# Q and K of two heads stacked in the partitions, scores from 64-row matmuls on both halves of the array

## The chip, the cores and the metric

One core of a Trainium2 chip runs the whole program. The metric is device time in microseconds (us); the time before is the median of three runs. Engines are named as in the profile: PE is TensorE (PEld its weight loads), DVE is VectorE, ACT is ScalarE, POOL is GpSimd, SP is SyncE, which issues DMAs.

## The reference

Causal attention with a multiplicative decay, then two MLPs. Batch 4, 8 heads, 576 positions, head size 64; 2304 tokens, model width 512, hidden width 2048.

```python
scores = scale * np.matmul(q, k.transpose(0, 1, 3, 2))
cum = np.cumsum(np.log(np.clip(f, 0.0001, 1.0)), axis=-1)
scores = np.where(causal, -1000000000.0, scores + cum[:, :, :, None] - cum[:, :, None, :])
attn = np.exp(scores - np.max(scores, axis=-1, keepdims=True))
attn = attn / (np.sum(attn, axis=-1, keepdims=True) + 1e-09)
x = np.matmul(attn, v)          # heads side by side: 2304 x 512
h = x @ moe_w_in;  y = (h * sigmoid(1.702 * h)) @ moe_w_out
h = y @ moe2_w_in; out = (max(h, 0) + alpha * min(h, 0)) @ moe2_w_out
```

## The kernel before

Operands of a matmul are split into a high part, rounded to fp32r, and a low part, the rest; a product is then high x high + high x low + low x high, three fp32r matmuls in place of a plain fp32 one.

Attention runs in 32 units (`seq`, line 830). A unit is a pair of heads of one batch and a range of queries: the first sixteen have queries 0 to 256, the others 256 to 576 (320 queries, keys 0 to 576). `prep` (line 479) loads q and k so that 64 partitions hold q's head dimension and the other 64 k's, both heads side by side in the free dimension; DVE transposes blocks of 32x32, one instruction per head (line 496). ACT casts the high parts, DVE or POOL subtracts the low ones (helpers at lines 343 and 348), each on 64 partitions. KB and QB hold low above high and high above low, so one 128-row matmul gives two of the three products; KA and QA hold a second copy of the high parts in rows 0 to 63 and three more rows with cumulated decay, ones and the negated row maximum, so that a 67-row matmul gives the third product and all that is added to it.

`chunk` (line 568) finds the row maxima: for each query tile of 128 and each head one 66-row matmul (line 599), a masked max on DVE (line 602), and then a transpose of the maxima on PE (line 617), which ACT or DVE negate into QA (lines 625, 627). The last 64 queries of both heads share one tile through `z`. `chunk2` (line 632) computes transposed scores for each key tile (lines 654 and 655 for two heads in one PSUM bank, 666 and 667 with a bank for each head), exponentials on ACT (658, 670), a causal mask on POOL (674) and the products with v, in plain fp32 where there are at most 256 queries (lines 686, 692), else in split form (715). Line 686 puts two 64-column matmuls on the two column halves of the array (`tile_position=(0, r)`). Then come the normalisation and the write to xr (725 to 747).

As soon as the columns of 256 tokens are there, `mlp1a` (line 779) runs the first 8 of 16 hidden slots of the first MLP on them (lines 758, 800). It needs 8 converted weight slots (`weight`, lines 449 to 474). The other hidden slots (lines 758, 882) and the second MLP (758, 911) follow when the attention's buffers are free.

The order of all of this is made by a planner (`Plan`, line 69). Each operation has estimated costs on the engines that may run it, reads, writes and a priority; the planner picks, at each step, the operation that can start first, and priority only breaks ties. The result is one fixed order per engine. All eight PSUM banks are one pool; `ps_s` (scores, up to 3 banks), `ps_m` (maxima, 2), `ps_v` (output, 3), `ps_h` (hidden, 2) and `ps_y` (MLP output, 2) are only upper limits. All DMAs are issued by SP, in planned order, so a load that waits for its buffer holds back the ones behind it.

## Time and profile before

| | us |
|---|---|
| median of three runs (lowest, highest) | 1099.09 (1098.65, 1100.13) |
| the profiled execution | 1101.62 |
| its span, first to last instruction | 1099.9 |
| PE busy | 1040.2 |
| DVE busy | 745.8 |
| ACT busy | 503.7 |
| POOL busy | 129.1 |

Busy time of PE is of modelled, pipelined matmuls. What an engine is worth in a stretch is read from the stretch: its busy time there, the granted clock of PE, and what it waited for.

### The profile page before, as it was taken

To read this page: it belongs to the slowest core of one execution; us is meant where nothing else is said; L and a number is where in the kernel's file an instruction comes from. 1 tells how busy PE (TensorE), PEld (TensorE's weight loads), DVE (VectorE), ACT (ScalarE), POOL (GpSimd) and SP (SyncE) were. 2 spreads that over 40 slices of the span, in tenths; PEclk is the share of its full clock that TensorE was granted. 3 is DMA by queue.
4 is the path that set the end of the run, shared out by engine and by line. 5 is a ranking of instruction groups with operands and counts; after the bars stand their busy time and mean duration, and the time that the engine had idled before them with its cause. 6 is when DMAs were issued, how large, how long until landed. Compare 5 with 4: busy or idle time off the path is not lost.

```text
span 1099.9 us, 16292 instructions
## 1 busy us (share of the span) xinstructions
PE 1040.2 (95%) x5955; PEld 897.4 (82%) x5955; DVE 745.8 (68%) x1565; ACT 503.7 (46%) x1009; POOL 129.1 (12%) x179
## 2 busy tenths in 40 slices
PE   4797899999989899999999999999999999999997
PEld 2576888899978889998888898788888888898885
DVE  7998988998989888878973449833443434444433
ACT  6787756567667566667752337511210201211111
POOL 5331111213212221000100000300000000000000
PEclk7697898999979979999999999999999999999999
DMA  6555465344453330655653234500100200100001
GB/s 188 133 166 163 143 168 135 84 108 108 94 135 93 90 95 12 201 184 151 215 179 105 77 103 149 170 1 1 67 1 1 68 1 1 34 24 20 1 1 39
DMA packets 86329, 101.95 MB, mean 93 GB/s; under 512 B 35496, under 2 KB 65384, under 8 KB 86248
## 3 DMA queue, kind: packets, MB, share of 16 engines
q1 hardware_dynamic: 86248, 100.90, 32.0%
q8 instruction: 47, 0.77, 0.3%
q14 instruction: 34, 0.28, 0.1%
HBM read 81.54 MB, written 19.02 MB: 91 GB/s over the span
## 4 chain that ended last, share of the span: by engine, by line
PE 70%; DVE 10%; issue 2%; DMA 2%; ACT 1%; SPq 0%; DVEq 0%; ACTq 0%
PE bk L758 30%; PE bk L911 17%; PE bk L882 8%; PE bk L800 5%; PE bk L715 3%; PE bk L666 2%; PE bk L599 2%; PE bk L667 1%; DVE bk L602 1%; DVE T L496 1%; DVE KB L348 1%; DVE el L348 1%; DVE tr L728 1%; PE bk L655 1%; PE bk L686 1%
## 5 line engine op out<-in xcount | busy, mean ns | idle before, releaser
L343 ACT CAST qgh<-qgg 128x512 fp32r<-128x512 f32 (+1 forms) x120 | 69.3, 578 | 338.3 <-DVE qgg L772 314.8
L769 DVE TENSOR_SCALAR qgg<-bk,alpha_sb 128x512 f32<-128x512 f32 (+1 forms) x80 | 55.5, 695 | 166.9 <-PE bk L758 166.9
L758 PE MATMUL bk<-qx,wB 128*128 128x512 f32 (+1 forms) x720 | 156.9, 370 | 0.0
L758 PEld LDWEIGHTS bk<-qx,wB 128*128 128x128 f32 x720 | 125.8, 188 | 24.5
L758 PE MATMUL bk<-xh,wA 128*128 128x256 f32 x576 | 125.2, 297 | 3.1 <-ACT wA L343 2.0
L348 DVE TENSOR_TENSOR qgl<-qgg,qgh 128x512 fp32r<-128x512 f32 (+1 forms) x116 | 75.5, 651 | 67.3 <-ACT qgh L343 58.7
L758 PEld LDWEIGHTS bk<-xh,wA 128*128 128x128 f32 x576 | 100.8, 202 | 5.3 <-ACT wA L343 2.2
L758 PE MATMUL bk<-qx,wA 128*128 128x512 f32 (+1 forms) x480 | 104.3, 369 | 0.0
L758 PEld LDWEIGHTS bk<-qx,wA 128*128 128x128 f32 x480 | 83.9, 188 | 16.4
L602 DVE CUSTOM_DVE_ANT_0 bk<-bk,mask 128x512 f32<-128x512 f32 (+3 forms) x160 | 75.9, 495 | 14.5 <-PE bk L599 11.8
L758 PE MATMUL bk<-xl,wA 128*128 128x256 f32 x288 | 84.6, 294 | 1.1 <-DVE xl L348 1.1
L800 PE MATMUL bk<-gh,wA 128*128 128x256 f32 x576 | 83.7, 288 | 1.8 <-POOL wA L348 0.7
L800 PEld LDWEIGHTS bk<-gh,wA 128*128 128x128 f32 x576 | 76.1, 194 | 3.2 <-ACT gh L343 1.3
L911 PE MATMUL bk<-wA,qgh 128*128 128x512 f32 x288 | 73.7, 395 | 0.2 <-ACT qgh L343 0.2
L348 POOL TENSOR_TENSOR qx<-qxb,qx 128x512 fp32r<-128x512 f32 (+1 forms) x12 | 15.3, 1277 | 431.3 <-ACT qx L343 373.1
L911 PEld LDWEIGHTS bk<-wA,qgh 128*128 128x128 f32 x288 | 53.7, 188 | 13.1 <-ACT qgh L343 0.6
L496 DVE STREAM_TRANSPOSE T<-raw 128x256 f32<-128x256 f32 (+1 forms) x64 | 58.9, 940 | 3.3 <-DMA raw<-in_k_dram 3.0
L758 PEld LDWEIGHTS bk<-xl,wA 128*128 128x128 f32 x288 | 58.2, 202 | 1.6 <-DVE xl L348 1.5
L458 ACT ACTIVATE wc<-wraw 128x512 f32<-128x512 f32 x64 | 43.2, 678 | 27.6 <-DVE wA L348 9.3
L911 PE MATMUL bk<-wB,qgh 128*128 128x512 f32 x216 | 54.5, 392 | 0.0
L882 PE MATMUL bk<-qgh,wB 128*128 128x512 f32 (+1 forms) x240 | 54.3, 368 | 0.0
L758 PE MATMUL bk<-qx,wC 128*128 128x512 f32 (+1 forms) x240 | 53.0, 371 | 0.0
(150 smaller groups left out, 2129.3 us busy)
## 6 DMA issues: line engine op xcount, KB each, us to landing
wraw<-in_moe_w_in_dram SPq DMA_DIRECT2D x32, 512.0 KB
wraw<-in_moe_w_out_dram SPq DMA_DIRECT2D x32, 512.0 KB
xscr<-xr SPq DMA_DIRECT2D x9, 512.0 KB
ypscr<-yp SPq DMA_DIRECT2D x18, 256.0 KB
raw<-in_q_dram SPq DMA_DIRECT2D x16, 288.0 KB
raw<-in_k_dram SPq DMA_DIRECT2D x16, 288.0 KB
raw<-in_q_dram SPq DMA_DIRECT2D x16, 280.0 KB
raw<-in_k_dram SPq DMA_DIRECT2D x16, 280.0 KB
```

The lines of the kernel that those rows point to most:

```text
L343: nc.scalar.copy(dst, src)
L348: E[e].tensor_tensor(dst, a, b, op=ALU.subtract)
L458: plan.add([("ACT", c_act(n))], lambda e: nc.scalar.mul(w.ap, high().bitcast(F32), 2.0 ** -112), [raw], [w], pri)
L496: [("DVE", 1.9 * n)], lambda e, hh=hh: nc.vector.transpose(T.ap[:, hh, :n].rearrange("p (i n) -> p n i", n=nb), raw.ap[:, hh, :nb * D].rea ...
L599: nc.tensor.matmul(pm.ap[:rows, :c1 - c0], l, ka.ap[0:66, hh, c0:c1], start=hh == hhs[0], stop=hh == hhs[-1])
L602: plan.add([("DVE", c_dve(c1 - c0) + 90.0)], lambda e, pm=pm, rows=rows, c0=c0, c1=c1, mk=mk, m0=m0, col=col: nc.vector.tensor_tensor_redu ...
L715: nc.tensor.matmul(pb[hh].ap[:l.shape[1], s0 - q0:n], l, rhs.ap[:w, hh, :m], start=st, stop=sp, skip_group_check=True,)
L758: nc.tensor.matmul(ph.ap[:, :n], wb.ap[:, a, c, :], x(c), start=(c == 0 and i == 0), stop=(c == KT - 1 and i == 2))
L769: plan.add([("DVE", c_dve(n) + 56)], lambda e: nc.vector.tensor_scalar(g.ap[:, :n], ph.ap[:, :n], 0.0, alpha_sb[:, m:m + 1], op0=ALU.min, ...
L800: nc.tensor.matmul(py[d // 2].ap[:, d % 2 * BLK:(d % 2 + 1) * BLK], W1[m].ap[:, a, KT + d, :], g.ap, start=(m == 0 and i == 0 and a == 0 a ...
L882: nc.tensor.matmul(py[d].ap[:, :n], W1[m].ap[:, a, KT + d, :], g.ap[:, :n], start=(m == NA and i_ == 0 and a == 0), stop=(m == NM - 1 and ...
L911: nc.tensor.matmul(py[t].ap, g.ap[:, t * P:(t + 1) * P], wo[:, a, KT * P:], start=(m == 0 and i_ == 0 and a == 0), stop=(m == NM - 1 and i ...
```

## The change

Both heads of a pair are now stacked in the partitions: head 0 in 0 to 63, head 1 in 64 to 127. k and q get tiles of their own, loaded in four 32-partition DMAs each, with runs of 32 floats; only the unit's own queries of q are loaded. One unstrided transpose, one cast and one subtraction on 128 partitions handle k, and the same q. KH, KL, QH and QL hold the parts, three buffers each. DK and DQ hold, in three rows of each half, what is added to the scores (64 rows, the others zero). A score is four 64-row matmuls per head, in turns on the upper and the lower half of the partitions, into two PSUM banks, and each head has its own exponential. The row maxima are two 64-row matmuls per head in the same turns (the second has `ones` as weights); the shared last tile is two 128-row matmuls. The duplicates KA and QA go. The sums come in two DMAs instead of one for units after the fourth, and v's last rows in one instead of two. `ps_s` may have 4 banks. The loads of q and k of the first sixteen units may be issued by ACT. Initial fills run on POOL alone, and v's loads don't wait for them.

The core of the diff:

```diff
+QUEUE = {"SP": "SP", "ACTQ": "ACT"}
...
+    ACTQ = 16
...
-    p_qa = sb("att", "QA", 2, [67, 2 * (S - SPLIT)], F32R)
-    p_z = sb("att", "Z", 2, [66, 192], F32R)
-    p_ka = sb("att", "KA", 2, [67, 2, S], F32R)
-    p_QB = sb("att", "QB", 2, [P, 2, S - SPLIT], F32R)
-    p_KB = sb("att", "KB", 2, [P, 2, S], F32R)
-    p_raw = sb("att", "raw", 1, [P, 2, S * 2])
-    p_T = sb("att", "T", 1, [P, 2, S])
+
+    ones = att.tile([P, 2, P], F32R, name="ones")
+    p_z = sb("att", "Z", 2, [P, P], F32R)
+    p_rk = sb("att", "rk", 2, [P, S])
+    p_rq = sb("att", "rq", 2, [P, S - SPLIT])
+    p_tk = sb("att", "tk", 1, [P, S])
+    p_tq = sb("att", "tq", 1, [P, S - SPLIT])
+
+    p_kh = sb("att", "KH", 3, [P, S], F32R)
+    p_kl = sb("att", "KL", 3, [P, S], F32R)
+    p_dk = sb("att", "DK", 3, [P, S], F32R)
+    p_qh = sb("att", "QH", 3, [P, S - SPLIT], F32R)
+    p_ql = sb("att", "QL", 3, [P, S - SPLIT], F32R)
+    p_dq = sb("att", "DQ", 3, [P, S - SPLIT], F32R)
...
-    ps_s = psum_pool(3)
+    ps_s = psum_pool(4)
...
+    def set_ones(e):
+        nc.gpsimd.memset(ones.bitcast(F32), 0.0)
+        for hh in range(2):
+            nc.gpsimd.memset(ones[64 * hh:64 * hh + 2, 0].bitcast(F32), 1.0)
+            nc.gpsimd.memset(ones[64 * hh:64 * hh + 2, 1, 64 * hh:64 * hh + 64].bitcast(F32), 1.0)
+
+    b_one = Buf()
+    plan.add([("POOL", 600.0)], set_ones, (), [b_one], -87)
...
+        ("dk", p_dk, lambda x: (x.bitcast(F32), x[0:3].bitcast(F32), x[64:67].bitcast(F32)), 3 * S, (0.0, 1.0, 1.0)),
+        ("z", p_z, lambda x: x.bitcast(F32), P, 0.0),
+        ("dq", p_dq, lambda x: x.bitcast(F32), S - SPLIT, 0.0),
...
-            plan.add([("POOL", 0.95 * n + 60.0), ("DVE", n / 0.96 + 68.0)], lambda e, p=p, i=i, view=view, val=val: [
+            plan.add([("POOL", 0.95 * n + 60.0)], lambda e, p=p, i=i, view=view, val=val: [
...
-        for j, src in enumerate((q, k)):
-            for e_ in range(2):
-                o = 64 * j + 32 * e_
-                ln = nb * D - 32 * e_
-                plan.add(DMA(32 * 2 * ln * 4), lambda e, o=o, e_=e_, src=src, ln=ln: nc.sync.dma_start(
-                    raw.ap[o:o + 32, :, 0:ln],
-                    src[b, h0:h0 + 2, 0:n].rearrange("h (p n) d -> p h (n d)", n=nb)[:, :, 32 * e_:32 * e_ + ln],
+        m = n - q0
+        kh, kl, dk, qh, ql, dq = (Buf(x) for x in (p_kh, p_kl, p_dk, p_qh, p_ql, p_dq))
+        fdk, fdq = filled("dk", p_dk), filled("dq", p_dq)
+        for src, p_r, p_t, hi, lo, c0 in ((k, p_rk, p_tk, kh, kl, 0), (q, p_rq, p_tq, qh, ql, q0)):
+            raw, T = Buf(p_r), Buf(p_t)
+            w = n - c0
+            for o in range(0, P, 32):
+                hh, e_ = o // 64, o // 32 % 2
+                d_ = DMA(32 * w * 4 * 1.6)
+                if actq:
+                    d_.append(("ACTQ", d_[0][1], 300.0))
+                plan.add(d_, lambda e, src=src, hh=hh, e_=e_, o=o, raw=raw, w=w, c0=c0: E[e].dma_start(
+                    raw.ap[o:o + 32, 0:w].rearrange("p (n d) -> p n d", d=32),
+                    src[b, h0 + hh, c0:c0 + w, 32 * e_:32 * e_ + 32].rearrange("(n p) d -> p n d", p=32),
                 ), (), [(raw, o)], pri)
-        m = n - q0
-        for hh in range(2):
-            plan.add(
-                [("DVE", 1.9 * n)], lambda e, hh=hh: nc.vector.transpose(
-                    T.ap[:, hh, :n].rearrange("p (i n) -> p n i", n=nb),
-                    raw.ap[:, hh, :nb * D].rearrange("p (n d) -> p n d", d=D)[:, :, 0:32],
-                ), [raw], [(T, hh)], pri,
-            )
-        Tq, Tk = lambda: T.ap[0:64, :, q0:n], lambda: T.ap[64:P, :, :n]
-        Qh, Ql = lambda: QB.ap[0:64, :, :m], lambda: QB.ap[64:P, :, :m]
-        Kh, Kl = lambda: KB.ap[64:P, :, :n], lambda: KB.ap[0:64, :, :n]
-
-        def dup(dst, dap, src, sap, w):
-            def go(e):
-                if e == "SP":
-                    nc.sync.dma_start(dap().bitcast(F32), sap().bitcast(F32))
-                else:
-                    copy(e, dap(), sap().bitcast(F32))
-
-            plan.add([(*DMA(64 * 2 * w * 4)[0], BD), *a_copy(2 * w)], go, [src], [(dst, "h")], pri)
-
-        plan.add(a_copy(2 * n), lambda e: copy(e, Kh(), Tk()), [T], [(KB, "h")], pri)
-        plan.add(a_copy(2 * m), lambda e: copy(e, Qh(), Tq()), [T], [(QB, "h")], pri)
-        dup(ka, lambda: ka.ap[0:64, :, :n], (KB, "h"), Kh, n)
-        dup(qa, lambda: qv(qa.ap[0:64, 0:2 * qw]), (QB, "h"), Qh, m)
+            plan.add([("DVE", 1.13 * w + 70.0)], lambda e, raw=raw, T=T, w=w: nc.vector.transpose(T.ap[:, :w], raw.ap[:, :w]), [raw], [T], pri)
+            plan.add(a_copy(w), lambda e, T=T, hi=hi, w=w: copy(e, hi.ap[:, :w], T.ap[:, :w]), [T], [hi], pri)
+            plan.add(a_sub(w), lambda e, T=T, hi=hi, lo=lo, w=w: sub(e, lo.ap[:, :w], T.ap[:, :w], hi.ap[:, :w].bitcast(F32)), [T, hi], [lo], pri)
...
+            for i in range(2):
+                plan.add(DMA(8 * n), lambda e, i=i: nc.sync.dma_start(
+                    dkv()[:, i, :n].bitcast(F32), cscr[i, r:r + 2, :n]
+                ), [*((b_cum, (p_, i)) for p_ in parts), *fdk], [(dk, i)], pri)
...
+                pms = [Buf(ps_m) for _ in range(2 if w == P else 1)]
+
+                def mm(e, pms=pms, a=a, w=w, c0=c0, c1=c1):
+                    if w < P:
+                        o = pms[0].ap[:, :c1 - c0]
+                        nc.tensor.matmul(o, z.ap, kh.ap[:, c0:c1], start=True, stop=False)
+                        nc.tensor.matmul(o, ones[:, 1], dk.ap[:, c0:c1], start=False, stop=True)
+                        return
+                    for x, y in ((qh, kh), (None, dk)):
+                        for hh in range(2):
+                            r = slice(64 * hh, 64 * hh + 64)
+                            l = ones[r, 0, :w] if x is None else x.ap[r, a - q0:a - q0 + w]
+                            nc.tensor.matmul(pms[hh].ap[:, :c1 - c0], l, y.ap[r, c0:c1], start=x is not None, stop=x is None)
+
+                plan.add([("PE", 2 * c_mm(c1 - c0, P))], mm, [qh if w == P else z, kh, (dk, 0), (dk, 1), b_one, *u["fdk"]], pms, pri)
...
+                for g, hh in enumerate(hhs):
+                    def ev(e, i0=i0, i=i, a=a, w=w, hh=hh, g=g):
+                        d = dq.ap[64 * hh:64 * hh + 3, a - q0:a - q0 + w]
...
+            pss = [Buf(ps_s), Buf(ps_s)]
+
+            def sc(e, pss=pss, a=a, w=w, s0=s0, m=m):
+                for i, (x, y) in enumerate(((kh, qh), (kh, ql), (kl, qh), (dk, dq))):
                     for hh in range(2):
+                        r = slice(64 * hh, 64 * hh + 64)
+                        nc.tensor.matmul(pss[hh].ap[:w, :m], x.ap[r, a:a + w], y.ap[r, s0 - q0:n], start=i == 0, stop=i == 3)
+
+            plan.add([("PE", 4 * c_mm(m, w))], sc, [kh, kl, dk, qh, ql, dq], pss, pri)
+            for hh in range(2):
+                plan.add([("ACT", c_act(m, True))], lambda e, hh=hh, pss=pss, e32=e32, w=w, m=m: nc.scalar.activation(
+                    e32.ap[:w, hh, :m], pss[hh].ap[:w, :m], AF.Exp, scale=0.125
+                ), [pss[hh]], [(e32, hh)], pri)
```

## Rows read from the trace of the kernel before

**Rows 1.** The page: the span in 40 slices, tenths busy, tenths of full clock

```profile
DVE  7998988998989888878973449833443434444433
...
PEclk7697898999979979999999999999999999999999
```

**Rows 2.** Stretches: start:end, length, busy us of five engines, PE clock, DMA share, GB/s

```profile
0.00:165.00 165.00, 128.24 (x850) 106.83 (x850) 145.33 (x402) 116.71 (x235) 44.57 (x72) 0.81 0.58 160
165.00:443.00 278.00, 263.84 (x1919) 246.56 (x1921) 246.40 (x563) 177.51 (x390) 56.66 (x87) 0.94 0.38 94
443.00:493.50 50.50, 49.13 (x409) 48.56 (x407) 44.61 (x95) 36.20 (x78) 1.77 (x1) 1.00 0.65 209
```

**Rows 3.** An instruction of PE: start, length, line, idle before and what ended it

```profile
317.40 0.27 PE L617 MATMUL bk<-ident_r,MX 128*3 128x128 f32 x1 [2.54 <-DVE MX L609]
```

**Rows 4.** Groups of DVE: line, tiles, shapes, count, busy us, mean ns, idle before

```profile
L496 DVE STREAM_TRANSPOSE T<-raw 128x576 f32<-128x576 f32 x32 | 39.6, 1243 | 3.1 <-DMA raw<-in_k_dram 3.0
L348 DVE TENSOR_TENSOR KB<-T,KB 64x1152 fp32r<-64x1152 f32 x16 | 21.7, 1354 | 1.0 <-ACT KB L343 0.6
L496 DVE STREAM_TRANSPOSE T<-raw 128x256 f32<-128x256 f32 x32 | 19.3, 637 | 0.2
L348 DVE TENSOR_TENSOR QB<-T,QB 64x640 fp32r<-64x640 f32 x16 | 13.1, 819 | 0.4
L348 DVE TENSOR_TENSOR KB<-T,KB 64x512 fp32r<-64x512 f32 x16 | 12.4, 777 | 1.1 <-ACT KB L343 0.8
```

**Rows 5.** Groups of DVE with the shapes nearest to the new ones

```profile
L348 DVE TENSOR_TENSOR el<-e,eh 128x640 fp32r<-128x640 f32 x43 | 35.7, 835 | 4.3 <-ACT eh L343 4.0
L348 DVE TENSOR_TENSOR gl<-gg,gh 128x256 fp32r<-128x256 f32 x47 | 20.3, 436 | 1.7 <-ACT gh L343 1.0 <-PE bk L800 0.5
L735 DVE STREAM_TRANSPOSE tr<-rc 128x320 f32<-128x320 f32 x16 | 7.9, 495 | 0.1
L735 DVE STREAM_TRANSPOSE tr<-rc 128x256 f32<-128x256 f32 x16 | 6.8, 426 | 0.0
```

**Rows 6.** Groups of ACT

```profile
L670 ACT ACTIVATE e<-bk 128x320 f32<-128x320 f32 x96 | 35.7, 443 | 9.9 <-PE bk L667 9.6
L343 ACT CAST KB<-T 64x1152 fp32r<-64x1152 f32 x16 | 18.5, 1154 | 0.3
L658 ACT ACTIVATE e<-bk 128x512 f32<-128x512 f32 x16 | 9.5, 596 | 5.6 <-PE bk L655 5.4
```

**Rows 7.** DMA: two stretches as in rows 2; issues of line 489 (min/median/max ns)

```profile
205.50:208.50 3.00, 3.00 (x21) 2.77 (x21) 2.57 (x6) 2.98 (x6) 2.88 (x4) 1.00 0.97 239
195.50:196.50 1.00, 1.00 (x10) 1.00 (x10) 1.00 (x4) 0.00 (x0) 1.00 (x2) 1.00 0.86 195
...
L489 SPq DMA_DIRECT2D raw<-in_k_dram x64: 311/425/1404, 1.7 to 389.8; - x64
```

**Rows 8.** Instructions of PE in order of time, at full clock

```profile
123.39 0.28 PE L758 MATMUL bk<-xh,wA 128*128 128x256 f32 x1
123.60 1.52 PE L686 MATMUL bk<-e,VR 128*64 128x256 f32 x16
125.05 0.39 PE L599 MATMUL bk<-KA,QA 66*128 66x256 f32 x1
...
185.15 0.31 PE L666 MATMUL bk<-QA,KA 67*128 67x320 f32 x1
185.30 0.31 PE L667 MATMUL bk<-QB,KB 128*128 128x320 f32 x1
...
186.42 0.27 PE L655 MATMUL bk<-QB,KB 128*128 128x192 f32 x1
186.53 0.28 PE L654 MATMUL bk<-QA,KA 67*128 67x192 f32 x1
...
191.63 0.81 PE L692 MATMUL bk<-e,VR 128*128 128x192 f32 x4
192.37 0.45 PE L686 MATMUL bk<-e,VR 64*64 64x64 f32 x8
```

More of the change, by code (lines that the diff above doesn't have):

```diff
@@ L127, in run @@
                     bias, port = (*more, 0.0, False)[:2] if len(more) < 2 else more
-                    t = max(t0, free.get(eng, 0.0))
+                    t = max(t0, free.get(QUEUE.get(eng, eng), 0.0))
                     if port:
                         t = max(t, free.get("port", 0.0))
-                    if eng == "SP":
+                    if eng in QUEUE:
                         end = max(t + 1150.0, dma) + dur + 750.0
@@ L144, in run @@
             o.start, o.eng = t, eng
[L145 to L146 removed]
+            if eng in QUEUE:
+                free[QUEUE[eng]] = t + 480.0
                 dma = end - 750.0
@@ L216 @@
     plan = Plan()
-    E = {"PE": nc.tensor, "DVE": nc.vector, "ACT": nc.scalar, "POOL": nc.gpsimd, "SP": nc.sync}
+    E = {"PE": nc.tensor, "DVE": nc.vector, "ACT": nc.scalar, "POOL": nc.gpsimd, "SP": nc.sync, "ACTQ": nc.scalar}
     const = ctx.enter_context(tc.tile_pool(name="const", bufs=1))
@@ L578, in chunk @@
             jobs += [(j, t, a, w, (hh,)) for hh in range(2)] if w == P else [(j, t, a, w, (0, 1))]
-        for ji, (j, t, a, w, hhs) in enumerate(jobs):
+        ji = 0
+        for j, t, a, w in [(j, *x) for j, x in enumerate(tiles)]:
             ext = a + w
@@ new lines, in chunk @@
+                plan.add([("PE", 2 * c_mm(c1 - c0, P))], mm, [qh if w == P else z, kh, (dk, 0), (dk, 1), b_one, *u["fdk"]], pms, pri)
+                for i, pm in enumerate(pms):
+                    col = 32 * (ji + i) + (2 if c0 == 0 else 3)
+                    if w == P:
+                        mk, m0 = mask, 3 * P - t * P + c0
+                    else:
+                        mk, m0 = (mask, 0) if c1 < ext else (mask2, 0)
+                    plan.add([("DVE", c_dve(c1 - c0) + 90.0)], lambda e, pm=pm, c0=c0, c1=c1, mk=mk, m0=m0, col=col: nc.vector.tensor_tensor_reduce(
+                        pm.ap[:, :c1 - c0], pm.ap[:, :c1 - c0], mk[:, m0:m0 + c1 - c0], 1.0, NEG,
+                        ALU.add, ALU.max, accum_out=mx.ap[:, col:col + 1],
+                    ), [b_mask if mk is mask else b_mask2, *fmx], [pm, (mx, col)], pri)
+                    cols.append(col)
@@ L608, in chunk @@
+            if w < P:
                 x, y = cols
-                plan.add([("DVE", 70.0, 0.0, True)], lambda e, x=x, y=y, rows=rows: nc.vector.tensor_tensor(
-                    mx.ap[:rows, x:x + 1], mx.ap[:rows, x:x + 1].bitcast(F32), mx.ap[:rows, y:y + 1].bitcast(F32), op=ALU.max
+                plan.add([("DVE", 70.0, 0.0, True)], lambda e, x=x, y=y: nc.vector.tensor_tensor(
+                    mx.ap[:, x:x + 1], mx.ap[:, x:x + 1].bitcast(F32), mx.ap[:, y:y + 1].bitcast(F32), op=ALU.max
@@ L832 @@
     for i, (b, hp, q0, q1) in enumerate(seq):
-        unit = prep(b, hp, q0, q1, A0 + i - PRE, i < EARLY)
+        unit = prep(b, hp, q0, q1, A0 + i - PRE, i < EARLY, i < ACTQ)
         pend.append((chunk(unit, q0, q1, A0 + i), col0(b, q0) + q1 - q0 if hp == NP - 1 else 0))
```

120 lines of the change are left out of this document (33 added, 87 removed).

## The prediction

> **What bounds the kernel now.** I began with the page's slices: TensorE (PE) runs at full granted clock in nearly all of the later ones, while the first half shows VectorE (DVE) at seven to nine tenths through the first nineteen and PE's clock below full again and again [rows 1]. So there are two kernels in one, and only the first is touched. I cut it into four stretches [rows 2]: A, 0 to 165 us, about the first sixteen units (256 queries); B, to 443 us, the last of the sixteen units with 320 queries; C, to 493.5 us, the rest of the first MLP part, for which PE needs no more attention; then D, the 606 us that are left, MLP alone at full clock [rows 1]. D does not change. C is PE's as well (busy for 49.1 of 50.5 us), so the end of the kernel is D plus whatever it takes PE to get through all work of A, B and C.
>
> What does that work take? In A PE is idle for 165.0 - 128.2 = 36.8 us, and its mean clock of 0.81 costs roughly another 165 x 0.19 = 31 us; so its work is worth about 97 us at 2.4 GHz. In B it is idle for 14 us and the clock costs 278 x 0.06 = 17 us: 247 us of work. C has 49. Together 393 us of work in 493.5: 68 us are lost in A, 33 in B and C. Who makes PE wait? DVE is busy for 88% of A and 89% of B, ScalarE (ACT) for 71% and 64% [rows 2]. A typical loss in B, at 317 us: PE waits 2.54 us for DVE's last row maximum [rows 3], and the slice that follows has a clock of 0.7 in place of 0.9 or more [rows 1]. A is DVE's stage; B is one where PE and DVE are both close to full.
>
> **DVE: what goes and what comes.** Now, per unit of the first kind, two strided transposes of 128x256 (0.637 us each) and two subtractions of 64x512 (0.777 for K; Q has the same shape); of the second kind two of 128x576 (1.243) and two subtractions (1.354 and 0.819) [rows 4]. That is 2.83 and 4.66 us. Afterwards the same values lie on all 128 partitions: transposes of 256 and 256, or 576 and 320 columns, unstrided, and subtractions of the same widths. Unstrided 32x32 transposes take 0.426 (256) and 0.495 us (320); for 576 I extend the line, 0.495 + 256 x 1.08 ns = 0.77. Subtractions take 0.436 (256 columns) and 0.835 (640) [rows 5]; between them 320 gives 0.52 and 576 gives 0.75. So 2 x 0.43 + 2 x 0.44 = 1.73 us and 0.77 + 0.50 + 0.75 + 0.52 = 2.54: 1.10 and 2.12 us less per unit, 17 us in A and 34 in B. In A DVE's share of the initial fills, which I put at 5 us, also moves to GpSimd, idle for 120 of A's 165 us; in B some 4 us come back, from two small copies into z per unit in place of one and one more copy of maxima. DVE's work: A 145 - 22 = 123, B 246 - 30 = 216.
>
> **ACT.** K of a second unit is cast as 64x1152 in 1.154 us [rows 6] and then copied once more for KA; Q likewise, 64x640, by columns some 0.7 each: 3.7 us. One cast of 128x576 and one of 128x320, half the columns each and so about 0.6 to 0.7 and 0.4, replace all four: 2.6 us less per second unit and, by columns, 1.6 less per first one, 67 us in all. Every exponential that covered both heads is split: 0.596 for 512 columns becomes two of 256, which the line through that and 0.443 for 320 puts at 0.39 [rows 6]; 0.19 more, over four such tiles per pair of units and 16 pairs some 10 us. ACT may also issue loads in the first sixteen units. Its price is not in the trace; SP's row has a median of 0.425 us per load [rows 7]. At most half of 128, 64 x 0.42 = 27 us, if none hides behind a running instruction, and nothing if all do. I take 13: ACT in A is then 117 - 26 + 5 + 13 = 109, below DVE. What is queued behind such a load, should it wait for its buffer, are exponentials and casts, and PE behind those; two buffers make that wait rare.
>
> **Loads.** The loads of q and k move 26.1 MB now (both operands, both heads, 256 or 576 rows of 256 bytes, less the 32 columns that the second of two loads skips), at 239 GB/s and a share of 0.97 where they run alone [rows 7]: 26.1 / 0.239 x 0.97 = 106 us of all engines. Afterwards a run is 32 floats, 128 bytes: 4 x 512 runs per first unit, 4 x 896 per second, 90,112 in all. The nearest row is v's: 256-byte runs at 195 GB/s and a share of 0.86 [rows 7], 0.86 x 16 / 762 = 18 ns each. A run of half the size costs between nothing and that, so at most 90,112 x 18 / 16 = 101 us. No dearer than now, and spread over 380 us. Issues: eight instead of four of 0.42 us per unit, and the rows of sums as two instead of one; SP has some 17 us for a second unit (B over 16). At the start v's loads no longer wait on SP for their fill; the rows don't price that, it stays at nothing and no loss, since a wait goes. A load that waits for its buffer still holds back the ones behind it, weights among them.
>
> **PE.** Now a score tile is two full-height matmuls per head: from one start to the next 0.15 us at 320 columns (0.133 at 2.4 GHz and about 0.014 more, 0.147) and 0.11 at 192 [rows 8]; for 64 I take 0.06. Afterwards it is four 64-row matmuls per head, and the row maxima are two instead of one. If the upper and the lower half run at once, a pair costs what one full matmul did and the sum stays. The rows have no row halves, but they have column halves: the 16 matmuls of line 686 for one unit, two for each of the code's four per key tile, 8 of 256 columns and 8 of 128. They are plain fp32 and stream their columns twice: line 692, fp32 and full height, takes 0.74 us for four of 192 columns, 0.185 each, where fp32r takes 0.11 [rows 8]. One after another at 2.4 GHz that is (8 x 512 + 8 x 256) / 2.4 = 2560 ns, 2.56 us; they took 1.45 until the next line starts. So halves do run in pairs, 1.28 us of it, and 0.17 us is lost on the way in and out; the matmul of 256 columns ahead took 0.21 instead of 0.107 + 0.014 = 0.12, another 0.09. A visit to split mode costs 0.26 us. Bounds for the overlap: none (the pairs' time doubles) to 14 ns less per pair than now (147 against 320/2.4 = 133). I take the row of the column halves, full overlap, worth -4 us. What the pairs stream per unit is, second kind, 12 x 0.147 + 4 x 0.11 + 4 x 0.06 + 2 x 0.175 + 2 x 0.23 = 3.25 us, first kind 4 x 0.12 + 4 x 0.11 + 2 x 0.11 + 2 x 0.12 = 1.38: 74 us over all, so overlap matters.
>
> The Trainium skill, "TensorE: Matmul & The Clock Gate", Part 3, gives a measured 3.07 times for four row tiles, so 77% of ideal; it speaks against full overlap. By it the 74 us would grow by 0.3 x 74 = 22 (an estimate from that page), some 16 of it in B, where the sum would come out at 1098; the row of line 686 shows 2.0 for two column halves once the visit is taken off.
>
> How many visits? A second unit has two max steps and five score steps in pairs; scores that follow one another share a visit. Four PSUM banks for scores let two steps stand side by side, so 3 to 7; I take 6. First units: 2 to 4, I take 3.5. A: 56 x 0.26 = 15 us, B: 96 x 0.26 = 25; ends 8 to 17 and 12 to 29.
>
> **The sum.** A is DVE's: 123 / 0.88 = 140, 25 us shorter (10 if only the chain through the maxima counts, 33 if the loads help). PE's 97 + 15 fit in it. B and C: PE has 296 + 25 - 4 = 317 us of work. DVE could finish B in 216 / 0.89 = 243 us, so DVE no longer holds B; PE does. It lost 33 us there; with DVE 12% lighter I take 20 (10 to 33). So 337 instead of 328.5, 8 us longer: PE pays for the visits and DVE's gain in B hardly shows. Net -25 + 8 = -17. The profiled execution took 1101.62 (span 1099.9), 2.5 above the median of 1099.09; both less 17: 1085 and **1082**. Its own range, from the ends of visits and losses: 1064 to 1096.
>
> **Rivals.** First, a larger gain: visits are cheap or few (12 us in B) and PE's loss falls to 10; then B and C take 314, 14 us less, and A 33 less: 1052. For it: in C, with DVE no longer ahead of it, PE was busy for 49.1 of 50.5 us [rows 2]; against: a second unit has seven steps that each want two banks.
>
> Second, slower: the halves do not overlap, or their weight loads come one after another. The pairs' 16 x 3.25 = 52 us in B then go on top (A has 28 us to spare for its 22): 1082 + 52 = 1134. With only the loads in turn, a pair cannot be under 2 x 0.11 (the 0.11 of a 192-column matmul is more than its 192/2.4 = 0.08, so its weights set it [rows 8]): 12 x 0.073 + 4 x 0.11 + 4 x 0.06 = 1.6 us per unit, 25 in B: 1107. It ends slower than before from about 17 us of extra PE work in B on. Against it stands the row of line 686.
>
> Third, PSUM. A max step and a score step now take two banks at once. The MLP accumulators hold two banks and the output of a unit two, so four are left. A score bank was held for 0.30 + 0.44 us, now for 0.60 + 2 x 0.44 = 1.5; the pair of max banks for both reductions. If steps queue for banks, PE idles as in [rows 3] more often: half of A's gain goes (12), B's loss stays at 33 (13): 1107. For it: DVE's reductions of one step can no longer overlap the next step's matmuls. The Trainium skill, "TensorEngine Tiling (Array Packing)", Gotcha 1, says that row tiles may not share a bank, which is why there are two; no row here shows it.
>
> Fourth, loads late: SP's order or ACT's loads stall DVE's transposes. DVE's transposes wait 3.0 us in all for loads now [rows 4]; up to 1 us per unit would be 16 us: 1098.
>
> **How the numbers follow.** Forecast 0.46; larger gain 0.20; no overlap 0.12; banks 0.14; loads 0.08. About 0.2%, 2 us, can be told from no change. Faster: 0.46 + 0.20 and 0.04 from banks and loads, 0.70. Same: 0.08, from those two. Slower: no overlap, and what is left of the two, 0.22. Range 1045 to 1118: it leaves out the best of the larger gains (0.07) and full serialisation (0.08) with a little of the banks.
>
> **What would show it.** Right: transposes at 0.43 to 0.8 us and DVE near 123 us of a shorter A; pairs of 64-row matmuls starting within some ns of each other, and 0.14 us per pair at 320 columns; B and C near 335 us with PE full. Wrong: a pair at 0.22 or 0.29 us; PE idle ahead of the max or score lines on DVE or ACT by more than before; DVE waiting for raw; the granted clock lower in B. The end of the first MLP part at 477 us, against 493.5, would be the sum itself.

## The result, and the profile after

The changed kernel takes 1089.13 us (median; 1084.09 to 1090.33) against 1099.61 us for the kernel before on the same chip: a ratio of 0.9893, with a 95% interval from 0.9857 to 0.9928, so about 1% faster (10.5 us between the medians of four runs each, 11.8 by the ratio). The profiled execution took 1090.33 us with a span of 1088.6, 11.3 us less than the one before. The last matmul of the first MLP part (line 793) ends at 481.4 us; before it was 493.5 (line 800). So all of the gain, 12.1 us in this pair of traces, is in the stretches that the forecast called A, B and C, and the rest is unchanged (607 us, was 606), as it should be.

The slices of the page after, and the three stretches (columns as in rows 2):

```profile
DVE  5878887788879875969963459743534333544433
...
PEclk8887899999999999999999999999999999999999
```

```profile
0.00:165.00 165.00, 128.29 (x1029) 103.88 (x1030) 126.29 (x401) 91.83 (x242) 48.03 (x94) 0.88 0.59 135
165.00:443.00 278.00, 274.83 (x2402) 247.81 (x2402) 225.43 (x581) 155.75 (x433) 51.61 (x83) 1.00 0.28 63
443.00:493.50 50.50, 50.50 (x375) 48.40 (x374) 41.22 (x86) 34.76 (x73) 0.24 (x1) 1.00 0.58 176
```

Beside [rows 1, 2] three things stand out. DVE is lighter in A (126 us, was 145) and in B (225, was 246), about as forecast (123 and 216). Yet PE's idle time in A is 36.7 us, and was 36.8. And in B PE is now busy for 274.8 of 278 us at full clock, where it had lost 14 us to idle time and some 17 to the clock. Worked out as in the forecast, PE's loss in A went from 68 only to 56 us (36.7 idle and 165 x 0.12 for the clock), that in B and C from 33 to 3, and PE's work grew by 29 us, from 393 to 422 (481.4, where the first MLP part ends, less 60). 41 less lost and 29 more work are the 12 us.

The new instructions of DVE (line, tiles, shapes, count, busy us, mean ns), and in B the longest waits of PE, for the maxima and for their negation into QA (total, times, longest), first of the kernel before and then of the changed one:

```profile
L514 DVE STREAM_TRANSPOSE tk<-rk 128x576 f32<-128x576 f32 x16 | 12.1, 757 | 0.0
L357 DVE TENSOR_TENSOR KL<-tk,KH 128x576 fp32r<-128x576 f32 x12 | 9.8, 819 | 0.4 <-ACT KH L352 0.3
L514 DVE STREAM_TRANSPOSE tq<-rq 128x320 f32<-128x320 f32 x16 | 8.0, 502 | 0.0
L514 DVE STREAM_TRANSPOSE tk<-rk 128x256 f32<-128x256 f32 x16 | 6.9, 429 | 0.7 <-POOL KL L357 0.6
```

```profile
PE bk L617 <- DVE MX L609: 5.9, 4, 2.5
PE bk L666 <- ACT QA L625: 3.0, 5, 1.0
PE bk L654 <- DVE QA L627: 2.1, 1, 2.1
PE bk L666 <- DVE QA L627: 1.6, 3, 1.3
```

```profile
PE bk L623 <- DVE MX L614: 1.1, 2, 0.8
```

The instructions answer to [rows 4] and cost about what was forecast from [rows 5] (0.77, 0.75, 0.50, 0.43). The 2.54 us wait of [rows 3] has no counterpart left. Of the 14 us that PE was idle in B, 12.6 were waits in the chain through the maxima; 1.1 us of these are left, and no wait for the negated maxima is among B's any more.

PE in the middle of B: start, length, line, operands, shape, count of the group (the two matmuls of a pair start within some 10 ns of each other and stand in one line):

```profile
289.36 0.28 PE L751 MATMUL bk<-xl,wA 128*128 128x256 f32 x1
289.48 0.28 PE L751 MATMUL bk<-xh,wA 128*128 128x256 f32 x1
289.69 0.44 PE L598 MATMUL bk<-KH,QH 64*128 64x384 f32 x2
289.96 0.34 PE L598 MATMUL bk<-DK,ones 64*128 64x384 f32 x2
290.14 0.31 PE L659 MATMUL bk<-QH,KH 64*128 64x320 f32 x2
290.29 0.30 PE L659 MATMUL bk<-QL,KH 64*128 64x320 f32 x2
...
291.88 0.40 PE L598 MATMUL bk<-KH,QH 64*128 64x512 f32 x2
...
293.07 0.39 PE L751 MATMUL bk<-xh,wA 128*128 128x256 f32 x1
```

Twelve pairs of 320 columns take 291.88 - 290.14 = 1.74 us, 0.145 each: a pair costs what one full-height matmul did [rows 8], so here the halves overlap fully. Going in is seen too: 0.21 us from the last matmul on full height to the first pair, where 256 columns take 0.12.

Last, the weights of the first MLP. First the kernel before, then after: SP's loads of them, and the casts that end the conversion of each half slot (count, min/median/max ns, first and last start):

```profile
L454 SPq DMA_DIRECT2D wraw<-in_moe_w_in_dram x11: 368/384/569, 3.1 to 141.9; - x11
L343 ACT CAST wA<-wc x15: 597/617/621, 13.1 to 114.6; 128x512 fp32r<-128x512 f32 x15
```

```profile
L471 SPq DMA_DIRECT2D wraw<-in_moe_w_in_dram x11: 385/408/792, 27.1 to 157.0; - x11
L352 ACT CAST wA<-wc x16: 601/619/631, 46.7 to 122.2; 128x512 fp32r<-128x512 f32 x16
```

This is one of two places where A's gain went (the other is full_height's, below). The first load of weights is issued at 27 us instead of 3, behind 24 loads of q and k on SP instead of 4, and the conversions begin at 47 instead of 13. The first six units are done by 60 us (71 before), but the next four take 12 to 18 us each, with eleven of the sixteen casts beside them. The sixteenth unit's row of line 728 (735 before) comes at 169 us, 8 earlier than before, while lines 751 and 793 have started 350 matmuls by 165 us instead of 390; 40 x 0.12 = 5 us of that is owed later. Three of the kernels below (in_turn, twice, twice_late) have nearly the same order in A; their traces give 166 to 170 us and 345 to 373 matmuls, so a single trace is good to a few us here.

### The profile page after: what moved, and what is told of

Read it like the earlier page. It is cut to its first block, busy times and chain, and to the rows that moved or that the text cites. A ratio compares the mean times of both kernels' runs of the same rounds, so it can differ in the third digit from the quotient of the medians.

```text
span 1088.6 us, 17737 instructions
## 1 busy us (share of the span) xinstructions
PE 1040.8 (96%) x6531; PEld 885.5 (81%) x6531; DVE 696.0 (64%) x1560; ACT 448.3 (41%) x1041; POOL 124.8 (11%) x196
## 3 DMA queue, kind: packets, MB, share of 16 engines
q10 hardware_dynamic: 10608, 1.28, 0.8%
## 4 chain that ended last, share of the span: by engine, by line
PE 69%; DVE 4%; ACT 1%; issue 1%; DMA 1%; SPq 0%; ACTq 0%
PE bk L751 30%; PE bk L904 18%; PE bk L875 8%; PE bk L793 5%; PE bk L659 3%; PE bk L708 2%; PE bk L598 1%; PE bk L685 1%; DVE wraw L480 0%; DVE wB L357 0%; PE bk L679 0%; DMA wraw<-in_moe_w_in_dram 0%; DVE wc L483 0%; DVE qgg L762 0%; DVE qgl L357 0%
## 5 line engine op out<-in xcount | busy, mean ns | idle before, releaser
L751 PE MATMUL bk<-xh,wA 128*128 128x256 f32 x576 | 122.6, 293 | 2.6 <-DVE wA L357 1.5
L751 PEld LDWEIGHTS bk<-xh,wA 128*128 128x128 f32 x576 | 95.7, 192 | 10.4 <-issue 3.8
L751 PE MATMUL bk<-xl,wA 128*128 128x256 f32 x288 | 81.9, 284 | 1.1 <-DVE xl L357 1.1
L663 ACT ACTIVATE e<-bk 128x320 f32<-128x320 f32 (+3 forms) x224 | 65.2, 365 | 29.9 <-PE bk L659 28.2
L751 PEld LDWEIGHTS bk<-xl,wA 128*128 128x128 f32 x288 | 55.4, 192 | 1.3 <-DVE xl L357 1.3
L667 POOL TENSOR_SCALAR_AFFINE_SELECT e<-e 128x256 f32<-128x256 f32 (+1 forms) x80 | 32.7, 421 | 199.4 <-ACT e L663 175.8
```

The source lines that it names most:

```text
L663: plan.add([("ACT", c_act(m, True))], lambda e, hh=hh, pss=pss, e32=e32, w=w, m=m: nc.scalar.activation(e32.ap[:w, hh, :m], pss[hh].ap[:w, ...
L667: plan.add([("POOL", 150.0 + 0.82 * 2 * w, 0.0, True)], lambda e, e32=e32, w=w: nc.gpsimd.affine_select(e32.ap[:w, :, :w], e32.ap[:w, :, : ...
L751: nc.tensor.matmul(ph.ap[:, :n], wb.ap[:, a, c, :], x(c), start=(c == 0 and i == 0), stop=(c == KT - 1 and i == 2))
```

## The experiments

Each kernel ran beside the kernel before on its chip. Times are set against the changed kernel by these ratios: the difference of two ratios times 1100 us. The changed kernel's own interval is 4 us to each side, and with the other kernel's a difference is good to 4 or 5 us; smaller ones are not told apart. full_height, in_turn, twice, twice_late and long_runs keep the planned order. In the others the edit lets the planner make another order for all engines, so more changes than the edit names.

| kernel | median us | ratio, 95% interval | against the changed kernel, us |
|---|---|---|---|
| changed | 1089.13 | 0.9893 [0.9857, 0.9928] | |
| full_height | 1066.91 | 0.9712 [0.9682, 0.9742] | -20 |
| in_turn | 1090.90 | 0.9916 [0.9884, 0.9948] | +3 |
| two_banks | 1098.00 | 0.9974 [0.9959, 0.9989] | +9 |
| twice | 1090.74 | 0.9891 [0.9872, 0.9910] | 0 |
| twice_late | 1097.27 | 0.9957 [0.9938, 0.9977] | +7 |
| w1_first | 1083.20 | 0.9843 [0.9824, 0.9862] | -6 |
| sp_only | 1097.30 | 0.9971 [0.9956, 0.9986] | +9 |
| long_runs | 1079.18 | 0.9789 [0.9768, 0.9810] | -11 |
| w1_first_sp_start | 1087.22 | 0.9860 [0.9836, 0.9884] | -4 |
| w1_first_long_runs | 1078.09 | 0.9791 [0.9770, 0.9812] | -11 |
| w1_first_stay | 1078.85 | 0.9783 [0.9766, 0.9800] | -12 |
| w1_first_stay_long | 1094.19 | 0.9947 [0.9928, 0.9967] | +6 |

**What a visit to split mode costs: full_height.**

```diff
-                    for hh in range(2):
-                        r = slice(64 * hh, 64 * hh + 64)
-                        nc.tensor.matmul(pss[hh].ap[:w, :m], x.ap[r, a:a + w], y.ap[r, s0 - q0:n], start=i == 0, stop=i == 3)
+                    nc.tensor.matmul(pss[i % 2].ap[:w, :m], x.ap[:, a:a + w], y.ap[:, s0 - q0:n], start=i < 2, stop=i > 1)
```

(The maxima likewise.)

> The changed kernel with each pair of 64-row matmuls replaced by one full-height matmul of the same columns (the scores of a pair of heads are summed, and the two banks share the four terms, so the values are other ones); all other instructions and their order stay. It leaves out the visits to the split mode and nothing else. If a visit costs 0.26 us and there are 96 of them from 165 to 443 us, as forecast, the end of the kernel comes 25 us earlier there, about 1064 against 1089. If the visits are as many and as dear as the trace of the changed kernel suggests (61 in that stretch, about 0.2 us each, so 12 us), about 1077. If the visits are hidden, or if a pair costs less than a full-height matmul, 1089 or more. From 0 to 165 us PE is idle for 37 us, so there I expect no more than 3 us from it.

It took 20 to 22 us less. PE's order in the changed kernel has 91 visits, 30 in A and 61 in B (forecast: 56 and 96), so a visit costs 0.22 to 0.24 us of the kernel's time, good to 0.05. My price was 0.26; the count was what I had too high. And visits in A are not covered by idle time: the first MLP part ends at 458.6 instead of 481.4 us, 23 us for 91 visits, 0.25 each with those of A among them. What PE saves in A goes to MLP matmuls that then need not be done later: 396 of them have started by 165 us instead of 350, and the sixteenth unit's row comes at 160 us instead of 169. A and B of this kernel:

```profile
0.00:165.00 165.00, 125.64 (x888) 103.73 (x888) 130.54 (x422) 94.00 (x248) 50.78 (x96) 0.91 0.62 141
165.00:443.00 278.00, 273.73 (x2155) 263.31 (x2156) 238.53 (x606) 169.37 (x465) 52.06 (x81) 0.99 0.31 77
```

Worked out as above, PE's loss is 54 us in A, about the 56 of the changed kernel, and 7 in B instead of 3. So in B some 4 us of what PE saves are lost again to waits and the clock, and the visits cost PE itself somewhat more than this price. The weights come as late here as in the changed kernel (first load at 27 us), so late weights alone do not explain A.

**Whether the halves overlap, and how firmly: in_turn.**

```diff
-                for i, (x, y) in enumerate(((kh, qh), (kh, ql), (kl, qh), (dk, dq))):
-                    for hh in range(2):
+                for hh in range(2):
+                    for i, (x, y) in enumerate(((kh, qh), (kh, ql), (kl, qh), (dk, dq))):
```

(The maxima likewise.)

> The changed kernel with the same 64-row matmuls in another order: within a step all of the upper head's, then all of the lower head's, so that neighbours use the same half of the array. If the two halves really stream at the same time in the changed kernel, that is lost here but for one pair at each turn: about half of the pairs' 3.25 us comes on top for each of the 16 second units, 52 us from 165 to 443 us, less some 10 for the neighbours at the turn, and up to 22 us before that, of which idle PE hides most: 1130 to 1150. If the halves did not overlap, and starts 3 ns apart in the trace were only an artefact of the records, the order makes no difference: 1089.

I was wrong by 40 us or more, and not because the halves don't overlap. PE in this kernel, columns as above:

```profile
290.46 0.45 PE L598 MATMUL bk<-KH,QH 64*128 64x384 f32 x2
...
290.92 0.30 PE L659 MATMUL bk<-QH,KH 64*128 64x320 f32 x1
291.06 0.30 PE L659 MATMUL bk<-QL,KH 64*128 64x320 f32 x1
291.10 0.41 PE L659 MATMUL bk<-QH,KH 64*128 64x320 f32 x1
291.21 0.30 PE L659 MATMUL bk<-QH,KL 64*128 64x320 f32 x1
291.35 0.30 PE L659 MATMUL bk<-QL,KH 64*128 64x320 f32 x1
291.36 0.31 PE L659 MATMUL bk<-DQ,DK 64*128 64x320 f32 x1
...
294.41 0.39 PE L751 MATMUL bk<-xh,wA 128*128 128x256 f32 x1
```

In program order the upper half's four (QH,KH; QL,KH; QH,KL; DQ,DK) come before the lower half's first. But the lower half's QH,KH starts at 291.10, ahead of the upper half's third and fourth (291.21, 291.36): in these rows each half takes its own matmuls in order and does not wait for the other's. The whole visit, two max steps and five score steps, takes 3.95 us here (290.46 to 294.41) and 3.38 in the changed kernel (289.69 to 293.07); one after another on 2.4 GHz its 6656 columns per head would need 2 x 6656 / 2.4 = 5.5 us. So the halves still overlap for the most part, and over the whole kernel the order costs nothing that can be told (+3 us, two runs). The Trainium skill, "TensorE: Matmul & The Clock Gate", Part 3, says that matmuls start strictly in program order without reordering; between two row halves this trace shows otherwise, by 0.1 to 0.3 us.

**PSUM banks: two_banks.**

```diff
-    ps_s = psum_pool(4)
+    ps_s = psum_pool(2)
```

> The changed kernel with two instead of four PSUM banks for the scores, so that no score step can stand beside another one. The rival that steps queue for banks would see its price here: every step waits for the exponentials of the one before (two of 0.3 to 0.45 us), PE changes modes at each of a second unit's steps, some 6 to 7 visits instead of 3.8, 16 x 3 x 0.25 = 12 us from 165 to 443 us, and PE's idle time rises: 1100 to 1115. If four banks are no more than two need, 1089.

Slower by 9 us, a little short of the range. Its stretch B:

```profile
165.00:443.00 278.00, 276.44 (x2346) 240.59 (x2345) 217.99 (x572) 160.56 (x433) 49.98 (x79) 1.00 0.28 63
```

PE is no more idle than in the changed kernel. What rises is the count of visits, from 91 to 118: at full_height's price 27 x 0.23 = 6 us of the 9. So too few banks seem to cost by scattering the score steps, and only little by making PE wait; the rest of the 9 us is not assigned.

**Is A the stage of DVE's throughput? twice, and the same in B: twice_late.**

```diff
-            ... lambda e, raw=raw, T=T, w=w: nc.vector.transpose(T.ap[:, :w], raw.ap[:, :w]) ...
+            ... lambda e, raw=raw, T=T, w=w: [nc.vector.transpose(T.ap[:, :w], raw.ap[:, :w]) for _ in range(2 if not q0 else 1)] ...
```

(`if q0` in twice_late.)

> The changed kernel with each of the 32 transposes of the sixteen first units issued twice (the second writes the same values again): 32 x 0.43 = 13.8 us more on VectorE between 0 and 165 us, the order of everything else kept. If VectorE's throughput bounds that stage, as the forecast had it, the time grows by 13.8 or a little more: 1103 to 1106. My theory now is that it doesn't (VectorE is busy for 126 of 165 us there): most of it goes into holes, and what stands in the chain of a unit counts: 1091 to 1096.

> The changed kernel with each of the 32 transposes of the sixteen second units issued twice (the second writes the same values again): 16 x (0.76 + 0.50) = 20 us more on VectorE, nearly all of it between 165 and 443 us, so that VectorE is as busy there as in the kernel before (245 of 278 us). If PE's loss in that stretch went from 33 to 3 us because VectorE got lighter, a good part comes back: PE idle for 8 us or more there and a clock below 0.97, time 1097 to 1110. If it went because operands are now ready earlier (three buffers, work ahead) and PE's queue never runs dry, VectorE's 33 idle us take it: 1089 to 1092.

In twice, DVE's groups of transposes, and stretch A:

```profile
L514 DVE STREAM_TRANSPOSE tk<-rk 128x256 f32<-128x256 f32 x32 | 14.0, 437 | 1.5 <-POOL KL L357 0.6 <-DMA rk<-in_k_dram 0.3
L514 DVE STREAM_TRANSPOSE tq<-rq 128x256 f32<-128x256 f32 x32 | 13.9, 433 | 0.7
```

```profile
0.00:165.00 165.00, 128.82 (x1024) 102.60 (x1024) 138.64 (x433) 91.91 (x241) 48.35 (x94) 0.89 0.59 135
```

14 us more work on DVE, and no difference in time that can be told. DVE is busy for 77% of A in the changed kernel and for 84% here. So its throughput does not bound A in the changed kernel; that rules out the forecast's reading of the stage after the change, and even my expectation of a few us was too high. The kernel before, with DVE busy for 88%, was not run in this way. In B it is otherwise. In twice_late 20 us more cost 7, good to 4 or 5, and in its trace PE waits more for DVE's maxima (4.2 us in five waits, was 1.1 in two) and is idle for 7.7 us of B instead of 3.2 (B, then the longest of PE's waits in it):

```profile
165.00:443.00 278.00, 270.31 (x2340) 241.53 (x2339) 233.09 (x590) 152.06 (x423) 48.82 (x80) 1.00 0.26 58
```

```profile
PE bk L623 <- DVE MX L614: 4.2, 5, 1.8
```

So DVE's lightness is worth some of what B gained. It is hardly all: PE's clock stays at 1.00, where I expected less than 0.97, and the 30 us don't come back. But the test is not quite a full one, since DVE is busy for 233 us of B here, not for the 245 that I expected and the 246 of the kernel before, and the traced execution (1093.9 us) is one of the faster ones. The others that changed with it (ACT lighter by 22 us in B, three buffers, the order) were not taken apart.

**The weights of the first MLP: w1_first, sp_only, w1_first_sp_start.** In this order:

```diff
-        plan.add(DMA(P * n * 8), lambda e: nc.sync.dma_start(raw.ap.rearrange("p c n t -> p c (n t)"), src), (), [raw], pri)
+        plan.add(DMA(P * n * 8), lambda e: nc.sync.dma_start(raw.ap.rearrange("p c n t -> p c (n t)"), src), (), [raw], pri - 5.5)
...
-    ACTQ = 16
+    ACTQ = 0
...
-        unit = prep(b, hp, q0, q1, A0 + i - PRE, i < EARLY, i < ACTQ)
+        unit = prep(b, hp, q0, q1, A0 + i - PRE, i < EARLY, EARLY <= i < ACTQ)
```

> The changed kernel with one number changed: the loads of the MLP weights get a priority 5.5 lower, so that the first two go out right behind the operands of the first two units, as in the kernel before, and not at 27 us. My theory of the first stage as it stands after the comparison of the traces: VectorE is not what bounds it any more; the conversions of the first MLP weights start at 47 us instead of 13 (their loads stand behind more loads of q and k on SP's queue) and all 16 then fall between 47 and 122 us, so that the units there take 13 to 18 us and PE lacks MLP work to fill its 37 idle us. Then this gives back most of what was missing: the end of the first MLP part goes from 481.6 to about 470 us, and the time to about 1078. Rival: the stage is bound by the chain through the maxima and VectorE whatever the order of conversions: 1087 to 1091. Second rival: the early weight loads delay q and k: units are late at the start, 1092 to 1096.

> The changed kernel with no loads on ScalarE's queue (39 of them in the first stage go to SP instead). If SP's queue is what holds back the weights and with them the first stage, 39 x 0.42 = 16 us more on SP make it worse: 1093 to 1100, the first conversion later than 47 us. If the loads that ScalarE issues are what delays the start (the first logarithm and the casts stand behind them; the first unit ends at 32 us instead of 29), it gets better by about 3 us: 1086. If neither, 1089.

> The changed kernel with the weights' loads early (as in w1_first, 1083) and with ScalarE issuing loads only from the fifth unit on. In sp_only the first logarithm started at 3.7 us instead of 8.6 and the first unit was done at 23 instead of 32 us, but the weights came later still and the sum was worse by 8. If these are two separate causes, both gains add: first unit at 23 to 25 us, first conversion before 30 us, end of the first MLP part 465 to 470, time 1075 to 1080. If the early units are not on the path, because PE's work is what the end waits for and the start only moves idle time, 1081 to 1085.

Loads and casts in w1_first, then in sp_only:

```profile
L471 SPq DMA_DIRECT2D wraw<-in_moe_w_in_dram x11: 368/386/1898, 7.7 to 145.1; - x11
L352 ACT CAST wA<-wc x15: 602/620/647, 19.6 to 116.9; 128x512 fp32r<-128x512 f32 x15
```

```profile
L471 SPq DMA_DIRECT2D wraw<-in_moe_w_in_dram x11: 372/385/1702, 55.1 to 161.6; - x11
L352 ACT CAST wA<-wc x15: 607/619/644, 63.5 to 126.7; 128x512 fp32r<-128x512 f32 x15
```

The order of the three is the order of the times: first load at 8 us, 1083; at 27, 1089; at 55, 1097. On SP 9, 24 and 64 loads of q and k stand ahead of it. The two ends are 14 us apart, well clear of noise; w1_first's own 6 us are only just clear of it. In w1_first the first MLP part ends at 471.9 us (481.4), PE is busy for 135.2 us of A instead of 128.3, and 393 of the first MLP's matmuls have started by 165 us instead of 350. The end of that part came as expected (about 470 us), the time, 1083 for 1078, did not quite. In sp_only, inside its range, SP's queue carries the 39 loads that ACT issues otherwise. It also shows what loads on ACT's queue do at the start. The table load ahead of ACT's first logarithm, and the first exponentials, in the changed kernel and then in sp_only:

```profile
7.29 1.28 ACT L422 ACT_TABLE_LOAD   x1 [3.94 <-DMA rq<-in_q_dram]
25.20 0.38 ACT L663 ACTIVATE e<-bk 128x256 f32<-128x256 f32 x1
```

```profile
2.42 1.28 ACT L422 ACT_TABLE_LOAD   x1
16.65 1.00 ACT L663 ACTIVATE e<-bk 128x256 f32<-128x256 f32 x4
```

The logarithm stands behind loads that ACT has to issue, and the first unit is done at 32 us instead of 23. But w1_first_sp_start, which frees ACT for the first four units, has its first unit at 23 us and is no better than w1_first: 1087, above both of its expected ranges. SP's queue then carries those loads, the conversions begin at 26 us instead of 20, and the sixth unit ends at 71 us in both. So the earlier start by itself bought nothing that can be told.

**The price of 128-byte runs: long_runs and w1_first_long_runs** (the second with w1_first's edit too).

```diff
-                    raw.ap[o:o + 32, 0:w].rearrange("p (n d) -> p n d", d=32),
-                    src[b, h0 + hh, c0:c0 + w, 32 * e_:32 * e_ + 32].rearrange("(n p) d -> p n d", p=32),
+                    raw.ap[o:o + 32, 0:w],
+                    src[b, h0 + hh, c0:c0 + w, :].rearrange("(p n) d -> p (n d)", p=32)[:, 0:w],
```

> The changed kernel with the same loads of q and k in count and bytes, but each partition reads one contiguous run of 1 to 2.3 KB in place of runs of 128 bytes (the operands then hold other elements of q and k, so the values are other ones). It takes the packets of these loads from about 155,000 to under 10,000 and leaves all else in place. If the price of short runs holds anything up (transposes that wait for loads, weights behind them), the first stage gets shorter: 5 us or more, 1084 or less. My theory: the loads are two units ahead, and only a wait or two for them goes: 1086 to 1089.

> w1_first (1083) with the long runs of long_runs in the loads of q and k (so other elements of q and k are read and the values are other ones). long_runs gained 10 us, w1_first 6 to 7. If both do the same thing by two ways, bringing the first MLP weights to their conversions sooner, the second gain is mostly used up: 1079 to 1083. If the early loads and the short runs are two causes (the start of the conversions, and the pace of loads behind them), they add up: 1071 to 1075.

DMA queues of the changed kernel, then of long_runs (packets, MB, share of 16 engines over the span), with the latter's casts:

```profile
q1 hardware_dynamic: 159360, 84.13, 28.7%
q10 hardware_dynamic: 10608, 1.28, 0.8%
```

```profile
q1 hardware_dynamic: 86176, 84.13, 26.6%
q10 hardware_dynamic: 1872, 1.28, 0.4%
```

```profile
L352 ACT CAST wA<-wc x16: 606/619/646, 46.6 to 112.5; 128x512 fp32r<-128x512 f32 x16
```

The same bytes in 81,920 fewer packets take 27.0% of 1077.1 instead of 29.5% of 1088.6, 291 instead of 321 us of all engines: 30 x 16 / 81,920 = 5.9 ns for each short run more. I had expected next to nothing of it, since DVE hardly waits for these loads; it is worth 11 us. What comes sooner is the end of the conversions, 112.5 instead of 122.2 us, though they begin at the same time. That end alone does not name the cause: in full_height, with the same loads, it is early too, its last cast of that first group starts at 114.6 us. With the weights' loads early as well nothing is added: 1078 and 1079. (Seen from w1_first, the long runs still add 5 or 6 us.) So the two edits seem to work mostly on one cause, the pace at which the first weights get through SP's queue and the DMA engines and are converted beside the units. That the queues' time and not some other effect of the runs does it follows from no run by itself. The Trainium skill, "DMA: Bandwidth & Descriptors", Why small descriptors are slow (HBM only), tells of a fixed cost for each packet and each descriptor; the 5.9 ns agree with it in kind.

**A faster version: w1_first_stay, w1_first_stay_long.** The planner learns of the modes, on top of w1_first:

```diff
-                if best is None or (t, o.pri, end, o.seq) < best[0]:
+                kt = t + (STAY if eng == "PE" and mode > o.mode else 0.0)
+                if best is None or (kt, o.pri, end, o.seq) < best[0]:
...
+            if eng == "PE":
+                if o.mode > mode:
+                    end += VISIT
+                mode = o.mode
```

`mode` is 1 for the 64-row steps; STAY is 400 or 1000 ns, VISIT 200.

> The early weights' loads (w1_first, 1083) and a planner that knows of the visits: an operation on full height is put up to 400 ns behind a 64-row step that can start by then, and entering the split mode costs 200 ns in the plan. The order then has 62 visits instead of 89. At the 0.24 us that full_height gave per visit (22 us for 91) this is worth 27 x 0.24 = 6.5 us: 1076 to 1078. If waiting in the split mode costs PE as much as leaving it, or the grouping delays the steps that VectorE and ScalarE wait for, 1083 or more.

> w1_first_stay (1079, 62 visits) with 1000 ns instead of 400 as the time by which full-height work is put behind a 64-row step: 43 visits. By 0.24 us per visit 19 x 0.24 = 4.6 us less: 1074. But PE now may stand idle for up to 1 us in the split mode where it had MLP work to do; if that is worth more than the visits it saves, 1079 or more.

The first is the fastest kernel here that does the whole computation, 1078.85 us, 2.2% less than before. Against w1_first it gains 6.6 us by the ratios for 27 visits, 0.24 us each. That agrees with full_height's price, but is good only to 0.1 us each, and the rest of the order changed as well. The second has 19 visits fewer still and is 18 us slower. A and B of the first, then of the second:

```profile
0.00:165.00 165.00, 136.33 (x1122) 111.01 (x1123) 132.05 (x421) 94.93 (x250) 54.28 (x99) 0.91 0.61 139
165.00:443.00 278.00, 272.81 (x2399) 250.86 (x2398) 245.33 (x617) 169.85 (x464) 34.40 (x63) 0.99 0.33 82
```

```profile
0.00:165.00 165.00, 131.81 (x1052) 105.16 (x1052) 132.78 (x420) 92.38 (x245) 58.32 (x102) 0.89 0.62 140
165.00:443.00 278.00, 270.09 (x2358) 246.58 (x2359) 243.03 (x605) 171.98 (x462) 38.72 (x68) 1.00 0.35 85
```

PE is busy for 7 us less in these two stretches, and it now pauses inside the score steps: over the first MLP part the time from the starts of line 667's QH,KH to the next start on PE adds up to 36 us, and to 25 in the first. What each of these pauses waits for was not taken apart. Here a pause of up to 400 ns paid for a visit of 240, a full microsecond didn't.

## Why the prediction was right, and where it was not

Faster, 1082 forecast, 1089 measured, inside 1064 to 1096, the likeliest case's own range. But 17 was the sum of -25 in A and +8 in B and C, and the traces show about -4 (units 8 us earlier, 5 us of MLP work owed) and -8. Two steps missed by 21 and 16 us, in opposite directions; that the sum is only 7 us off is luck.

- **DVE's and ACT's prices**: right, from 0.43 us for the small transpose to 0.76 for the large one (0.77 forecast); the subtraction of 576 columns took 0.82 for 0.75 (the line between the two rows gives 0.77, and 0.50 for 320 columns; the sum is the same). A cast of 576 columns took 0.68 us, an exponential of 256 took 0.38. ACT issued 39 loads, not 64.
- **"A is DVE's: 123 / 0.88 = 140"**: this step failed. DVE's work in A fell as forecast, to 126 us, but A did not shrink with it: DVE's share fell to 77%, and 14 us more DVE work change nothing (twice). A busy share near 0.9 was taken for a bound, after the change too, without asking for the waits behind it. Whether DVE bound A in the kernel before stays open.
- **What A hangs on instead**: PE's visits, paid in full (30 x 0.23 = 7 us; see below), and the first MLP's weights. For the weights, the term that I set at nothing was SP's queue: I saw that eight loads in place of four stand in it, priced their issue only for B, where SP has 17 us per unit, and wrote of weights held back by loads without giving it a time. A first unit takes 4 to 6 us at the start; 27 instead of 3 us for the first load of weights was the result, with the loads of several units ahead of it instead of one unit's. Whether the number of loads or the second raw buffer (one before) lets so many go ahead was not taken apart. w1_first gives 6 us back.
- **Loads**: the bound of 101 us of all engines held. All DMA together went from 352 us (32.0% of 1099.9) to 321. Queue q10 carries only loads of q and k: its 10,608 packets took 0.8% of 1088.6 us, 13 ns each of one engine for a bound of 18, which makes about 73 us for all 90,112. A short run costs 5.9 ns more than the same bytes in a long one. (The 26.1 MB of the kernel before are 26,112 KB of 1024 bytes, so 26.7 MB and 109 us; nothing hangs on it.) The inference from there to "no loss" is what failed: 11 us (long_runs).
- **The fourth rival** had the right place, loads, and looked for the wrong symptom, DVE's transposes waiting for raw; these wait for no load in the changed kernel's rows. ACT does stand idle behind loads of q, five times and for 10.9 us in all, where I took such waits to be rare; no run shows a price for it.
- **Full overlap**: right, 0.145 us per pair for 0.133 to 0.147, and the second rival is out. It is sturdier than I thought (in_turn).
- **Visits**: the price right (0.22 to 0.25 for 0.26), the count too high: 61 for 96 in B, so 61 x 0.23 = 14 us for 25. In A the price is paid in full, where I let it fit into idle time.
- **PE's loss in B and C**: 33 to 20 was forecast, with 10 as the other end; it went to 3. From 165 us on the cold stretches of [rows 1] are gone, and PE hardly ever waits: in the chain through the maxima for 1.1 us of B instead of 12.6. DVE's lightness is worth about 7 us of it (twice_late); what the rest hangs on stays open. This is the condition of the first rival, the larger gain: its conditions for B and C came about (14 us of visits for 12, a loss of 3 for 10), with 8 us of its 14, its A did not. (The slice with a clock of 0.7 is the one in which the wait at 317 us falls, not the one that follows.)
- **Banks**: four are enough for PE hardly to wait in B; with two the price seems to be mostly visits.

## What to carry to other kernels

Before calling an engine the bound of a stretch, look for the waits behind it, or give it more to do: here its work fell by 19 us, the stretch gained some 4, and 14 us put back cost nothing that can be told. When a change doubles the number of loads, price what stands behind them in the queue, weights for a later stage above all, and not only their own consumers. Where matmuls on halves of the array mix with full-height ones, count the changes of mode and let the planner know of them; grouping them was worth a short pause here, not a long one.

## What the runs showed of the hardware that was not expected

Row halves of the array take their matmuls independently: with all of one head's four ahead of the other's in program order, the second head's first starts 0.26 us before the first head's last (in_turn), and the two streams still overlap for the most part (3.95 us for a visit against 3.38, and 5.5 one after another). A change from full height to 64-row pairs and back costs 0.22 to 0.25 us of the kernel's time (full_height). A run of 128 bytes costs 5.9 ns of one DMA engine more than the same bytes inside a long run (long_runs). And loads in ACT's own queue went with 3.94 us of idle time ahead of the table load of its first logarithm, which came at 7.29 us instead of 2.42 (sp_only).
